# A layout change in a fused attention and MLP kernel: q_p turned by VectorE and DMA from the ninth pair on

## The chip, the cores and the metric

The kernel runs on one core of a Trainium2 chip. The metric is the device time in microseconds of one execution, the median of several runs; smaller is better. Engines: PE is TensorE, PEld its weight loads, DVE is VectorE, ACT is ScalarE, POOL is GpSimd, SP is the engine that issues all DMAs of this kernel.

## What is computed

Attention with positive random features for 8 x 8 (batch, head) slices of 576 tokens and 64 dimensions, and on its output, seen as 4608 tokens of 512 features, an MLP with 2048 hidden units and ELU. q, k, v and omega are fp32, the MLP's weights arrive as fp64.

```
scale = 1 / sqrt(sqrt(D))                       # D = 64, m = 128 features
phi(x): h = x @ omega.T - sum(x*x)/2            # x is q*scale or k*scale
        exp(h - max(h)) / sqrt(m)
q_p, k_p = phi(q * scale), phi(k * scale)       # [576, 128] per head
kv  = k_p.T @ v                                 # [128, 64]
z   = sum over tokens of k_p                    # [128]
num = q_p @ kv
den = q_p @ z + 1e-6
attn = num / den                                # -> x [4608, 512]
out  = elu(x @ w_in) @ w_out                    # [4608, 512] fp32
```

## The kernel before

**Pairs.** The attention is done in 32 pairs of two heads of one batch element, four pairs to a batch element. For pair i, `load_pair` issues the DMAs of k, q and v; `project` (once for k, once for q) makes the nine [128, 128] slices of k_p or q_p, tokens on partitions, in a tile `h` of shape [128, 9, 128]; `kv` makes kv (tile `kvf`) and the sums z; and `finish` does the rest. Of the nine slices of q_p, slices 0, 2, 4, 6 are the first 512 tokens of one head, 1, 3, 5, 7 those of the other, and slice 8 holds the last 64 tokens of both heads, one in each half of the partitions.

**The step that the change touches, `finish` (from L648).** pz (L664) spreads z over the partitions by a matmul. For three groups of slices (four, four, one) VectorE computes the denominators (L685) and reciprocals (L694), and POOL, or sometimes VectorE, multiplies q_p by them (`norm`, L696; the line shown in the profile is that of the helper, L359). Then the normalised q_p has to stand with features on partitions. Before, TensorE transposes each of the nine slices against an identity into PSUM tiles `pt` (L706), and ScalarE (or VectorE) copies each group out into `qh` [128, 2, 576] (L721; shown as L354). At last four matmuls (L733) multiply `kvf` by `qh`, one for each head and each of the token ranges 0..255 and 256..575, into two PSUM tiles `pn`; ScalarE writes the high part `xh` and VectorE the low part `xl` of x, features on partitions, into a ring of two batch elements, for the MLP. `qh` has one buffer, PSUM tiles of tag `pa` three, `h` four, and a tag `raw` (fp64 weights as they arrive, and the tile of the sums z) four.

**The MLP.** x is taken in 12 blocks of 384 tokens. A step of a block takes one of 16 slices of 128 hidden units: `layer1` (L864 to L866: high x high, high x low, low x high, for four feature chunks), ELU on ScalarE and VectorE, a split of the result in g (L882 to L891), and `layer2` (L902 to L904) into three PSUM accumulators. The first three blocks are run in two halves of 8 steps. A step's weights are converted from fp64 once, in the first block, stored to DRAM and loaded again by a DMA of 512 KB for each later step (`weights`, L839), into one of three buffers `w1c`.

**What sets the order.** No engine's order is written by hand. Every piece of work is a task with an engine (or alternatives), an estimated duration, a due time, and the buffers that it reads and writes (`Plan.op`). `Plan.order` runs a simulated clock: whenever an engine is free, it starts, of the tasks whose inputs are ready by that clock and for which buffers are free, the one with the earliest due time. The order so found is then issued, each engine's queue in that order; on the chip every instruction waits for its inputs by semaphores, in its place in the queue. In the plan a task on SP takes 500 ns per DMA, and its data land 1.1 us, plus the bytes at 360 per ns, plus 1.1 us after its start (L118, L244). `pair` (L752) sets the due times: a pair has a due time for its end, and its loads, projections, kv and last steps are due by fixed spans ahead of it. From the ninth pair on (i >= 8) these are the spans `LOAD2, K2, KV2, Q2`. The pairs of batch element b stand spread over the segment of the MLP ahead of the block that first needs them, four to a segment; PE takes MLP tasks and pair tasks in turn, by due time. The ninth to the thirty-second pair are computed while blocks of the MLP run.

Of the kernel before, what the change touches and what calls it, by code (L numbers as in the profile page):

```python
# [9 lines left out]
F32 = mybir.dt.float32  # L10
# [8 lines left out]
P = 128  # L19
B, H, S, D, M = 8, 8, 576, 64, 128  # L20
# [11 lines left out]
NJ = 9  # L32
# [18 lines left out]

PAIR0 = 9.46
DUE_LOAD, DUE_K, DUE_KV, DUE_Q = 27.64, 24.71, 14.12, 18.02
LOAD2, K2, KV2, Q2 = 56.0, 46.17, 30.64, 29.89
TAIL = 11.71
TAIL2 = 4.06

# [10 lines left out]
NHALF = 3  # L68

DUE_Z = 12.0  # L70


NONES = 8
# [27 lines left out]
class Plan:  # L101
# [21 lines left out]
    def op(self, eng, ns, due, fn, reads=(), writes=(), nbytes=0, alt=None, port=False, after=0.0):  # L123
        n = len(self.tasks)
        engs = {eng: (ns, 0.0)}
        for e, *t in alt or ():
            engs[e] = tuple(t)
        f = fn if alt is not None else lambda e: fn()
        deps, bufs = set(), set()
        for k in reads:  # L130
            if k in self.writer:
                deps.add(self.writer[k])
            self.readers.setdefault(k, []).append(n)
        for k in writes:
            if k in self.writer:
                deps.add(self.writer[k])
            deps.update(self.readers.pop(k, ()))
            self.writer[k] = n
        for k in (*reads, *writes):
            b = k[0] if isinstance(k, tuple) else k  # L140
            if isinstance(b, Buf):
                bufs.add(b)
        deps.discard(n)
        for b in bufs:
            b.left += 1
        self.tasks.append((engs, due, f, deps, bufs, nbytes, port, after))
# [135 lines left out]
def mm(n, m=1):  # L282

    return m * (n / 2.23 + 2.5)
# [6 lines left out]
def dve(n, fast=False):  # L291
    return 69 + n / (1.92 if fast else 0.96)
# [7 lines left out]
def performer_elu_kernel(  # L300
# [14 lines left out]
    nc = tc.nc  # L315
# [3 lines left out]
    sb = ctx.enter_context(tc.tile_pool(name="sb", bufs=1))  # L319
# [79 lines left out]
    def bank(i, early, name):  # L399

        tag = early if i < NEARLY else "pa"
        return Buf(ps, [P, 512], F32, tag, name, dict(pa=3, ph=2).get(tag, 1))

    def load_pair(i, due):
        s = st.setdefault(i, {})

        def dma(dst, src, nbytes, *writes):
            nonlocal due
            op("SP", 500, due, lambda: nc.sync.dma_start(dst(), src), (), writes, nbytes)
            due += 0.01  # L410

        for nm, nat, mixed in (("k", k, kx), ("q", q, qx)):
            if native(i, nm):
                t = s["x" + nm] = Buf(sb, [P, 2, S], F32, "ld" if nm == "k" else "t", f"x{nm}_{i}", 3 if nm == "k" else 2)
                dma(lambda t=t: t()[0:D], nat[i], 2 * P * S * 4, (t, 0), (t, 1))
            else:
                t = s["x" + nm] = Buf(sb, [P, 2, S], F32, "ld", f"x{nm}_{i}", 3)
                dma(lambda t=t: t(), mixed[i - NNAT[nm]], P * S * 8, (t, 0), (t, 3))
        t = s["v"] = Buf(sb, [P, NV], F32, "v", f"v_{i}", 2)
        dma(lambda: t(), v[i], P * NV * 4, t)  # L420

    def small(tag, n, name):
        return Buf(sb, [P, n], F32, tag, name, 2)
# [224 lines left out]
    def finish(i, due):  # L648

        s = st[i]  # L650
        h, z = s["hq"], s["z"]
        b, hp = divmod(i, NHP)
        den = small("den", NJ, f"den_{i}")


        pz = bank(i, "ph", f"pz_{i}")

        def spread():
            for a in range(2):
                nc.tensor.transpose(pz()[:, a * P:(a + 1) * P], z()[:, a:a + 1].to_broadcast([P, P]), ident)  # L660

        def sums():
            for e in range(2):
                nc.tensor.matmul(  # L664
                    pz()[:, 0:2 * M], ones, s["zr"]()[:, e * 2 * M:(e + 1) * 2 * M], start=(e == 0), stop=(e == 1)
                )

        if i < NONES:
            op("PE", 220, due - DUE_Z, spread, (z,), (pz,))
        else:  # L670
            op("PE", mm(2 * M, 2), due - DUE_Z, sums, ((s["zr"], "h"), (s["zr"], "l")), (pz,))
        qh = Buf(sb, [P, 2, S], F32, "qh", f"qh_{i}", 1)
        for g in range(3):
            d = due - 9 + g
            js = slice(4 * g, min(4 * g + 4, NJ))
            n = js.stop - js.start
            slots = [(j, j % 2, slice(0, P)) for j in range(4 * g, 4 * g + 4)]
            if g == 2:
                slots = [(8, a, slice(a * D, a * D + D)) for a in range(2)]
            hg = (h, g) if native(i, "q") else (h, min(g, 1))  # L680

            def dens(slots=slots):
                for j, a, r in slots:
                    junk = Buf(sb, [P, M], F32, "junk", f"junk_{i}_{j}_{a}", 2)
                    nc.vector.tensor_tensor_reduce(  # L685
                        out=junk()[r], in0=h()[r, j, :], in1=pz()[r, a * P:(a + 1) * P], scale=1.0, scalar=EPS,
                        op0=ALU.mult, op1=ALU.add, accum_out=den()[r, j:j + 1],
                    )

            def dg(js=js):  # L690
                return den()[:, js]

            op("DVE", len(slots) * 290, d, dens, (hg, pz), ((den, g),))
            op("DVE", 100, d + 0.5, lambda dg=dg: nc.vector.reciprocal(dg(), dg()), ((den, g),), ((den, g),))  # L694
            op(
                "POOL", 145 + 214 * n, d + 1.2,  # L696
                lambda e, js=js, n=n: tt(
                    e, h()[:, js], h()[:, js], den()[:, js].unsqueeze(2).to_broadcast([P, n, M]), ALU.mult
                ),
                (hg, (den, g)), ((h, "n", g),), alt=other("norm", "DVE", dve(n * M)), port=True,  # L700
            )
            p = bank(i, "pa", f"pt_{i}_{g}")

            def turn(g=g, p=p, js=js):
                for e, j in enumerate(range(js.start, js.stop)):
                    nc.tensor.transpose(p()[:, e * P:(e + 1) * P], h()[:, j, :], ident)  # L706

            def src(g=g, p=p):
                if g == 2:
                    return p()[:, 0:P].rearrange("p (a x) -> p a x", a=2)  # L710
                return p().rearrange("p (t a x) -> p a t x", t=2, a=2)

            def dst(x, g=g):
                if g == 2:
                    return x[:, :, 512:S]
                return x[:, :, g * 256:(g + 1) * 256].rearrange("p a (t x) -> p a t x", t=2)

            d = due - 5 + g
            op("PE", 109 * n, d, turn, ((h, "n", g),), (p,))
            op(  # L720
                "ACT", act(n * P, True), d + 0.5, lambda e, src=src, dst=dst: copy(e, dst(qh()), src()), (p,), ((qh, g),),  # L721
                alt=other("turn", "DVE", dve(n * P)),
            )
        kvf = kvs[i % 2]
        halves = [(slice(o, o + n), n, bank(i, "pa", f"pn_{i}_{o}")) for o, n in ((0, 256), (256, S - 256))]

        def mms():
            for qs, n, p in halves:  # L730
                for a in range(2):
                    r = slice(a * D, a * D + D)
                    nc.tensor.matmul(p()[r, 0:n], kvf[:, r], qh()[:, a, qs], start=True, stop=True)  # L733

        d = due - 2
        op("PE", 4 * mm(S) + 200, d, mms, [*((qh, g) for g in range(3)), ("kvf", i % 2)], [p for _, _, p in halves])
        for half, (qs, n, p) in enumerate(halves):
            xs = slice(qs.start + (b % 2) * S, qs.stop + (b % 2) * S)
            key = (b % 2, hp, half)
            op(  # L740
                "ACT", act(n, True), d + 0.8 + half, lambda e, xs=xs, n=n, p=p: copy(e, xh[:, hp, xs], p()[:, 0:n]),
                (p,), (("xh", key),), alt=other("x_hi", "DVE", dve(n)),
            )
            op(
                "DVE", dve(n), d + 1.2 + half,
                lambda xs=xs, n=n, p=p: nc.vector.tensor_tensor(  # L746
                    xl[:, hp, xs], p()[:, 0:n], xh[:, hp, xs].bitcast(F32), ALU.subtract
                ),
                (p, ("xh", key)), (("xl", key),),
            )  # L750

    def pair(i, due):  # L752

        at = (DUE_LOAD, DUE_K, DUE_KV, DUE_Q) if i < 2 * NHP else (LOAD2, K2, KV2, Q2)
        load_pair(i, due - at[0])
        project(i, "k", due - at[1])
        kv(i, due - at[2])
        project(i, "q", due - at[3])
        finish(i, due)


# [292 lines left out]
```

## Time and profile before

| | |
|---|---|
| timed runs | 1067.93, 1071.39, 1075.22 us; median 1071.39 |
| profiled execution, first to last instruction (span) | 1073.6 us |
| mean granted TensorE clock | 0.989 |
| busy: PE, ACT, DVE, POOL | 1046.5, 736.2, 605.4, 430.1 us |
| transposes of q_p (pt), nine a pair | 288 |
| matmul records of the final product (pn), eight a pair | 256 |
| DMA | 176.92 MB, mean 165 GB/s |

No separate device time is given for the profiled execution; its span lies within the range of the timed runs, 2.2 us above their median.

How to read the rows: a group of instructions stands as line, engine, operation, output<-inputs, shapes and count, then busy time in us and mean ns of one, then the engine's idle time ahead of it and what ended it. A matmul of fp32 operands is seen as two records, one of fp32r (the MLP's, the projections') or a transpose as one. Matmuls are pipelined, so the mean duration of one is longer than the step from one to the next; the chain's rows (start, us, what) show the steps. A wait's row tells who waited, for whom, us in total, how often, and the longest. A row of the windows view has the stretch, its length, busy us of each engine, the granted clock, the DMA engines' busy share and GB/s.

### The profile page before, as it was taken

What the parts mean: (1) busy time and instruction counts of PE and PEld (TensorE: products, weight loads), DVE (VectorE), ACT (ScalarE), POOL (GpSimd) and SP (SyncE); (2) the same over time, 40 slices, a digit from 0 to 9 for tenths busy, and PEclk for the clock granted to TensorE, in tenths of its full rate; (3) what the DMA queues carried; (4) which work ended last, traced back from release to release, by engine and by line L of the source; (5) the groups of instructions that cost most, each with busy time, mean ns of one, the idle gap of its engine ahead of it and who ended that gap; (6) DMA issues with size and microseconds to landing.
All of it is one profiled execution on the core that took longest, in us unless ns stands there. A gap on an engine that the chain in (4) does not pass through costs nothing.

```text
span 1073.6 us, 19168 instructions
## 1 busy us (share of the span) xinstructions
PE 1046.5 (97%) x6043; PEld 917.7 (85%) x6043; DVE 605.4 (56%) x2395; ACT 736.2 (69%) x1972; POOL 430.1 (40%) x440
## 2 busy tenths in 40 slices
PE   8989899999999999999999999999999999999998
PEld 7878789778888888998888888899888888899997
DVE  6898987684676764235556666224566665322221
ACT  6888775774878985347889988427889888432222
POOL 2446434234434563223455345323344454322221
PEclk8999899999999999999999999999999999999999
DMA  5666576558553553534544545443545542353431
GB/s 138 200 206 221 190 264 204 200 205 284 174 186 133 195 170 122 168 118 172 181 158 155 170 150 178 148 137 133 184 136 177 156 143 99 99 167 128 156 123 64
DMA packets 53238, 176.92 MB, mean 165 GB/s; under 512 B 6033, under 2 KB 6225, under 8 KB 53137
## 3 DMA queue, kind: packets, MB, share of 16 engines
q1 hardware_dynamic: 53136, 175.69, 49.5%
q8 instruction: 49, 0.80, 0.3%
q14 instruction: 53, 0.43, 0.1%
HBM read 155.48 MB, written 20.19 MB: 164 GB/s over the span
## 4 chain that ended last, share of the span: by engine, by line
PE 78%; ACT 8%; DVE 5%; DMA 3%; issue 2%; POOL 2%; SPq 0%; ACTq 0%; POOLq 0%; DVEq 0%
PE ph L864 11%; PE acc L902 10%; PE ph L866 10%; PE ph L865 10%; PE acc L903 10%; PE acc L904 10%; PE pn L733 3%; PE pt L706 3%; PE ppq L516 2%; ACT p2k L525 2%; DMA xq<-in_qx_dram 2%; PE pkv L608 2%; PE ppk L516 1%; ACT hk L436 1%; PE ppq L466 1%
## 5 line engine op out<-in xcount | busy, mean ns | idle before, releaser
L359 POOL TENSOR_TENSOR g<-e,g 128x384 fp32r<-128x384 f32 x176 | 187.3, 1065 | 430.9 <-DVE g L356 357.7
L864 PE MATMUL ph<-xh,w1c 128*128 128x384 f32 x768 | 266.4, 347 | 3.0 <-DVE e L877 1.6
L866 PE MATMUL ph<-xh,w1c 128*128 128x384 f32 x768 | 259.9, 338 | 0.9 <-DVE w1c L359 0.9
L865 PE MATMUL ph<-xl,w1c 128*128 128x384 f32 x768 | 259.3, 338 | 0.1
L877 DVE SCALAR_TENSOR_TENSOR e<-e,ph 128x384 f32<-128x384 f32 x192 | 106.2, 553 | 229.0 <-ACT e L874 221.6
L902 PE MATMUL acc<-w2h,g 128*128 128x512 f32 x576 | 231.5, 402 | 0.0
L873 ACT ACTIVATE e<-ph 128x384 f32<-128x384 f32 x192 | 94.4, 492 | 199.0 <-PE ph L866 195.4
L903 PE MATMUL acc<-w2l,g 128*128 128x512 f32 x576 | 227.2, 394 | 0.2 <-DVE w2l L359 0.2
L904 PE MATMUL acc<-w2h,g 128*128 128x512 f32 x576 | 225.5, 392 | 0.0
L864 PEld LDWEIGHTS ph<-xh,w1c 128*128 128x128 f32 x768 | 144.9, 189 | 18.3 <-issue 6.2
L865 PEld LDWEIGHTS ph<-xl,w1c 128*128 128x128 f32 x768 | 145.1, 189 | 7.3 <-DVE xl L746 0.4
L866 PEld LDWEIGHTS ph<-xh,w1c 128*128 128x128 f32 x768 | 144.7, 188 | 1.7 <-DVE w1c L359 1.5
L904 PEld LDWEIGHTS acc<-w2h,g 128*128 128x128 f32 x576 | 108.4, 188 | 24.4
L902 PEld LDWEIGHTS acc<-w2h,g 128*128 128x128 f32 x576 | 108.7, 189 | 16.7 <-issue 3.6
L903 PEld LDWEIGHTS acc<-w2l,g 128*128 128x128 f32 x576 | 108.7, 189 | 11.0 <-DVE w2l L359 0.5
L874 ACT ACTIVATE e<-e 128x384 f32<-128x384 f32 x192 | 101.4, 529 | 3.5
L534 DVE CUSTOM_DVE_ANT_0 hq<-ppq,p2q 128x128 f32<-128x128 f32 x216 | 54.6, 287 | 80.6 <-ACT p2q L525 70.3
L359 POOL TENSOR_TENSOR hq<-hq,den 128x512 f32<-128x512 f32 (+1 forms) x95 | 80.8, 866 | 45.8 <-DVE den L694 34.1
L525 ACT ACTIVATE p2q<-ppq,sqq 128x128 f32<-128x128 f32 x216 | 67.9, 373 | 21.3 <-PE ppq L516 20.9
L534 DVE CUSTOM_DVE_ANT_0 hk<-ppk,p2k 128x128 f32<-128x128 f32 x225 | 56.9, 287 | 40.4 <-ACT p2k L525 33.9
L685 DVE CUSTOM_DVE_ANT_0 junk<-hq,pz 128x128 f32<-128x128 f32 (+1 forms) x320 | 73.7, 280 | 8.7 <-PE pz L664 6.4
L812 POOL TENSOR_TENSOR u_w<-u_w,raw_w 128x512 int32<-128x512 int32 x32 | 44.9, 1405 | 81.6 <-DVE u_w L809 31.8
(96 smaller groups left out, 1613.2 us busy)
## 6 DMA issues: line engine op xcount, KB each, us to landing
w1c<-w1s SPq DMA_DIRECT2D x176, 512.0 KB, 3.3
raw_w<-in_w_dram SPq DMA_DIRECT2D x32, 512.0 KB, 4.6
xk<-in_kx_dram SPq DMA_DIRECT2D x25, 576.0 KB, 4.8
xq<-in_qx_dram SPq DMA_DIRECT2D x24, 576.0 KB, 4.2
v<-in_v_dram SPq DMA_DIRECT2D x32, 325.0 KB, 3.8
out_dram<-o SPq DMA_DIRECT2D x36, 256.0 KB, 3.6
w1s<-w1c SPq DMA_DIRECT2D x16, 512.0 KB, 3.0
xq<-in_q_dram SPq DMA_DIRECT2D x8, 288.0 KB, 4.2
```

What stands on the lines that cost most here:

```text
L359: (nc.vector if e == "DVE" else nc.gpsimd).tensor_tensor(*args)
L525: nc.scalar.activation(p2()[:, a], view()[:, a, M:], AF.Identity, bias=sq()[:, j:j + 1], scale=1.0)
L534: nc.vector.tensor_tensor_reduce(out=h()[:, j, :], in0=view()[:, a, 0:M], in1=p2()[:, a, :], scale=1.0, scalar=HIGHEST, op0=ALU.add, op1=A ...
L864: nc.tensor.matmul(ph(), wh, xh[:, c, o:o + TB], start=(c == 0), stop=False)
L865: nc.tensor.matmul(ph(), wh, xl[:, c, o:o + TB], start=False, stop=False)
L866: nc.tensor.matmul(ph(), wl, xh[:, c, o:o + TB], start=False, stop=(c == NC - 1))
L873: op("ACT", act(TB, True), due, lambda: nc.scalar.activation(e(), ph(), AF.Relu, scale=-1.0), (p,), (e,))
L874: op("ACT", act(TB), due + 0.2, lambda: nc.scalar.activation(e(), e(), AF.Exp, scale=-1.0), (e,), (e,))
L877: lambda: nc.vector.scalar_tensor_tensor(e(), e(), -1.0, ph(), ALU.add, ALU.max), (p, e), (e,),
L902: nc.tensor.matmul(a(), g()[:, 0, ts], w2h[:, f], start=(f == f0), stop=False)
L903: nc.tensor.matmul(a(), g()[:, 0, ts], w2l[:, f], start=False, stop=False)
L904: nc.tensor.matmul(a(), g()[:, 1, ts], w2h[:, f], start=False, stop=(f == f1 - 1))
```

## The change

For the pairs i >= 8 (`TURNED`) the nine transposes, their PSUM tiles and the copies are left out. In their place:

- One VectorE instruction transposes every 32 x 32 block of the nine normalised slices within itself, from `h` into a new tile `tb` [128, 1152] (tag `raw`), ordered so that the 288 columns that go to one group of 32 feature partitions are contiguous.
- Sixteen DMAs, from SBUF to SBUF, move blocks of [32 partitions, 288 columns] (36 KB) from token group n of `tb` to feature group m of `qh`. All 16 are issued on SP's queue, as four tasks of four.
- The columns of `qh` are now ordered by token group, slice and token within the group. The final product reads its tokens in runs of 32 through a strided pattern, and takes 256 columns at most: per head two matmuls of 256 columns and one of 64, where there were one of 256 and one of 320.
- The final product waits for the four move tasks in place of the three copies.
- Due times: the loads, both projections, pz, the denominators and the normalising of these pairs are due 7 us earlier (`EARLIER`); kv is due 33.0 in place of 30.64 us ahead of the pair's end. The end itself is due as before.

The first eight pairs and the MLP are not changed.

```diff
-LOAD2, K2, KV2, Q2 = 56.0, 46.17, 30.64, 29.89
+LOAD2, K2, KV2, Q2 = 56.0, 46.17, 33.0, 29.89
...
+TURNED = 8
+EARLIER = 7.0
+QB = 32
+NQB = P // QB
...
+        early = EARLIER if i >= TURNED else 0.0
...
-            op("PE", mm(2 * M, 2), due - DUE_Z, sums, ((s["zr"], "h"), (s["zr"], "l")), (pz,))
+            op("PE", mm(2 * M, 2), due - DUE_Z - early, sums, ((s["zr"], "h"), (s["zr"], "l")), (pz,))
...
-            d = due - 9 + g
+            d = due - 9 + g - early
...
+            if i >= TURNED:
+                continue
             p = bank(i, "pa", f"pt_{i}_{g}")
...
+        if i >= TURNED:
+            tb = Buf(sb, [P, NQB * NJ * QB], F32, "raw", f"tb_{i}", 4)
+
+            def blocks():
+                nc.vector.transpose(
+                    out=tb().rearrange("p (n j c) -> p j n c", n=NQB, j=NJ),
+                    in_=h().rearrange("p j (n c) -> p j n c", c=QB),
+                )
+
+            op("DVE", dve(NJ * M), due - 10, blocks, [(h, "n", g) for g in range(3)], (tb,))
+            for n in range(NQB):
+
+                def move(n=n):
+                    q = qh().rearrange("p a (n x) -> p (a n) x", n=2)
+                    w = NJ * QB
+                    for m in range(NQB):
+                        nc.sync.dma_start(
+                            q[m * QB:(m + 1) * QB, n], tb()[n * QB:(n + 1) * QB, m * w:(m + 1) * w]
+                        )
+
+                op("SP", 500 * NQB, due - 9, move, (tb,), ((qh, n),), QB * P * NJ * 4)
...
-                    nc.tensor.matmul(p()[r, 0:n], kvf[:, r], qh()[:, a, qs], start=True, stop=True)
+                    if i < TURNED:
+                        nc.tensor.matmul(p()[r, 0:n], kvf[:, r], qh()[:, a, qs], start=True, stop=True)
+                        continue
+                    q = qh().rearrange("p a (n j c) -> p (a n) j c", n=2, j=NJ)
+                    t = qs.start // P
+                    x = q[:, :, 2 * t + a:2 * t + a + 3:2, :].rearrange("p n j c -> p j n c")
+                    nc.tensor.matmul(p()[r, 0:2 * P], kvf[:, r], x, start=True, stop=True)
+                for a in range(2):
+                    if i >= TURNED and n > 2 * P:
+                        r = slice(a * D, a * D + D)
+                        nc.tensor.matmul(
+                            p()[r, 2 * P:n], kvf[:, r], q[:, 2 * a:2 * a + 2, 8, :], start=True, stop=True
+                        )
...
-        op("PE", 4 * mm(S) + 200, d, mms, [*((qh, g) for g in range(3)), ("kvf", i % 2)], [p for _, _, p in halves])
+        parts = range(NQB if i >= TURNED else 3)
+        op("PE", 4 * mm(S) + 200, d, mms, [*((qh, g) for g in parts), ("kvf", i % 2)], [p for _, _, p in halves])
...
-        load_pair(i, due - at[0])
-        project(i, "k", due - at[1])
+        load_pair(i, due - at[0] - (EARLIER if i >= TURNED else 0.0))
+        early = EARLIER if i >= TURNED else 0.0
+        project(i, "k", due - at[1] - early)
         kv(i, due - at[2])
-        project(i, "q", due - at[3])
+        project(i, "q", due - at[3] - early)
```

## The prediction

> **What bounds the kernel now.** I read the page first (busy shares and slices), then the windows view over the stages, then the waits, and last the chain and the timeline around single pairs.
>
> ```profile
> span 1073.6 us, 19168 instructions
> PE 1046.5 (97%) x6043; PEld 917.7 (85%) x6043; DVE 605.4 (56%) x2395; ACT 736.2 (69%) x1972; POOL 430.1 (40%) x440
> ```
>
> TensorE is busy for 97% of the span. A share of the whole span does not tell about a stage, so here are the windows that hold the pairs from the ninth on (their work lies between about 260 and 940 us):
>
> ```profile
> core 0: us, PE busy (x) PEld busy (x) DVE busy (x) ACT busy (x) POOL busy (x), PEclk, DMA share, GB/s
> 260.00:440.00 180.00, 179.65 (x1087) 155.52 (x1087) 108.85 (x515) 140.26 (x392) 78.49 (x83) 1.00 0.52 170
> 440.00:600.00 160.00, 158.95 (x928) 140.06 (x928) 81.78 (x371) 117.27 (x331) 63.89 (x68) 1.00 0.47 154
> 600.00:760.00 160.00, 159.13 (x908) 140.55 (x907) 76.81 (x332) 106.67 (x288) 60.72 (x65) 1.00 0.49 159
> 760.00:940.00 180.00, 178.41 (x1085) 154.30 (x1084) 102.39 (x516) 144.90 (x414) 82.94 (x91) 1.00 0.43 139
> ```
>
> The granted clock is 1.00 in all four, and PE's idle time is 0.35, 1.05, 0.87 and 1.59 us: 3.9 us in 680. So in this stage TensorE sets the pace. What is taken from it is gained, and any time it spends waiting is lost for good. VectorE has about half of each window free, and the DMA engines too.
>
> ```profile
> PE pt L706 <- POOL hq L359: 1.7, 6, 0.3
> PE pt L706 <- ACT qh L354: 1.4, 3, 0.5
> PE ppq L516 <- DVE mnq L534: 0.6, 1, 0.6
> PE ph L864 <- DMA w1c<-w1s: 0.5, 1, 0.5
> ```
>
> These are PE's waits from 250 us on: 3.1 of 4.2 us belong to the transposes that the change takes away, and the weight loads almost never make PE wait.
>
> **What is removed.** Nine transposes in each of 24 pairs are 216 instructions. The group's mean duration (first row below) overlaps with its neighbours, so I take the price from the chain, where only the step to the next matmul counts.
>
> ```profile
> L706 PE MATMUL pt<-ident,hq 128*128 128x128 f32 x288 | 50.2, 287 | 6.3 <-POOL hq L359 4.1 <-ACT qh L354 1.4 <-DVE hq L359 0.4
> 513.81 0.44 PE pt L706 x4
> 336.62 0.11 PE pt L706
> 333.58 1.24 PE pkv L608 x20
> 519.29 1.12 PE pn L733 x8
> ```
>
> 0.44 for four and 0.11 for one give 0.11 us each: 216 x 0.11 = **23.8 us**. With them go their two waits, **3.1 us**. ScalarE loses the copies out of PSUM, 24 x (2 x 590 + 276 ns) = 34.9 us, off the bound:
>
> ```profile
> L354 ACT COPY qh<-pt 128x512 f32<-128x512 f32 x64 | 37.7, 590 | 14.3 <-PE pt L706 14.0
> L354 ACT COPY qh<-pt 128x128 f32<-128x128 f32 x32 | 8.8, 276 | 1.9 <-PE pt L706 1.6
> ```
>
> That costs or gains nothing by itself; without that slack it would be worth 1.45 us a pair. The three PSUM banks of a pair that carried the transposes also fall free.
>
> **What is added on TensorE.** The final product had 2 x 256 and 2 x 320 columns per pair, seen as 8 records in 1.12 us. Now it has 4 x 256 and 2 x 64: the same 1152 columns in 12 records. The rows of 128 columns (pkv, 1.24 us for 20, so 0.062 us each) and of pn (1.12 us for 2304 columns in two passes, 0.49 ns a column) have the same price per column, so no fixed price is seen. Below: nothing extra. Above: a record of 64 columns costs as much as one of 128, 0.031 us more for each of four, 0.12 us a pair, 3.0 us in all. I take the middle, **1.5 us**. The moving operand is now read in runs of 32 floats; no row has that, so a full doubling stands among the rivals.
>
> **What is added elsewhere.** VectorE gets one transpose of 1152 columns per pair. The nearest rows:
>
> ```profile
> L356 DVE CAST g<-e 128x384 fp32r<-128x384 f32 x121 | 45.4, 375 | 23.4 <-PE acc L904 20.5
> L488 DVE TENSOR_REDUCE sqk<-xk 128x9 f32<-128x576 f32 x25 | 18.7, 748 | 12.5 <-ACT xk L485 12.4
> ```
>
> 375/384 and 748/576 ns a column make 1.1 to 1.5 us; I take 1.4. 24 of them are 34 us of VectorE, in windows where it is idle for 71 to 83 us each: nothing as busy time, but it counts in the path below. SP gets 16 issues of 36 KB each per pair, 24 x 0.59 = 14.2 MB. Issue, landing and volume now:
>
> ```profile
> 508.62 0.82 SPq L924 DMA_DIRECT2D out_dram<-o  x2
> 5.02 1.10 SPq L371 DMA_DIRECT2D omf<-in_omT_dram  x2
> 24.54 0.47 SPq L409 DMA_DIRECT2D xq<-in_q_dram  x1
> w1s<-w1c SPq DMA_DIRECT2D x16, 512.0 KB, 3.0
> w1c<-w1s SPq DMA_DIRECT2D x176, 512.0 KB, 3.3
> part<-o SPq DMA_DIRECT2D x9, 256.0 KB, 2.8
> SPq L839 <- PE ph L866: 425.1, 120, 9.6
> L864 PE MATMUL ph<-xh,w1c 128*128 128x384 f32 x768 | 266.4, 347 | 3.0 <-DVE e L877 1.6
> q1 hardware_dynamic: 53136, 175.69, 49.5%
> ```
>
> Two whole-tile stores back to back take 0.41 us each, two 64-row loads at the start 0.55, and one 64-row load alone 0.47. The moves have 32 rows, so I take 0.50, bounds 0.41 and 0.55. From issue to landing out of SBUF the trace has 3.0 us for 512 KB and 2.8 for 256. That bounds 36 KB from above at 3.0; half of it, 1.5, is the lower bound, and I take 2.4, a little under the line through both.
>
> The added volume is 8% of the 176 MB that now take half of the DMA engines' time: hidden. The moves wait on SP for the transpose, and behind them stand weight loads, the next loads of q, k, v and the stores. The weights have three buffers: SP spends 425 us waiting until a buffer is free, so a load is issued about two steps before its use, 2 x 1073.6/192 = 11 us (768 matmuls of L864, four a step, are 192 steps), and lands in 3.3. Sixteen issues, 8 us, would use up what is left only if all stood ahead of a load; the plan puts them by due times between loads. Price nothing; without that cover, up to a microsecond or two a pair. The loads, projections, sums and normalising that move 7 us earlier keep their instructions; their three loads per pair pass weight loads on SP, and the four h buffers are held longer. Price nothing, since PE waits for none of them now; in the ninth to twelfth pair, the closest ones, a few us if the buffers run out.
>
> **The step that decides: when the final product can start.** TensorE runs in the order that the plan wrote, so if the data of pn are late by the clock though not by the plan, PE stands, with the MLP matmuls (L864 to L904) queued behind pn.
>
> ```profile
> 559.98 1.40 POOL L359 TENSOR_TENSOR hq<-hq,den 128x512 f32<-128x512 f32 x2
> 563.96 0.27 ACT L354 COPY qh<-pt 128x128 f32<-128x128 f32 x1
> 565.41 1.19 PE L733 MATMUL pn<-qh,kvf 128*64 128x256 f32 x8
> 580.90 2.92 POOL L359 TENSOR_TENSOR hq<-hq,den 128x512 f32<-128x512 f32 x3
> 585.97 1.14 PE L733 MATMUL pn<-qh,kvf 128*64 128x256 f32 x8
> 604.47 1.41 POOL L359 TENSOR_TENSOR hq<-hq,den 128x512 f32<-128x512 f32 x2
> 612.40 1.19 PE L733 MATMUL pn<-qh,kvf 128*64 128x256 f32 x8
> ```
>
> From the end of the normalising to pn a middle pair of a batch has 4.0 us (561.38 to 565.41), the last one 2.1, the first one 6.5. New: transpose 1.4, hand-overs 0.3, fifteen more issues 7.5, landing 2.4: 11.6 us. The plan itself counts 1.3 for the transpose, 0.3 of hand-overs and 8.6 for the moves (four tasks of 2 us, the last ending 2.6 us after its start): 10.2. The chip is thus 1.4 us behind the plan. The chain starts 7 us earlier, so at its old place in PE's order pn would come 13.5 us after the normalising in a first pair, where the data are there; 11.0 in a middle one, where they are 0.6 late; and 9.1 in a last one, where the plan (10.2) must put pn later and the chip's 1.4 count, less the slack that the middle pair shows: its copy ends at 564.23, pn starts 1.18 later, and the plan asks for 0.27, so 0.9. PE stands 0.5 to 0.6 us; I take 0.5 for the 18 pairs that are not first in a batch: **9.0 us**. With the low ends (1.1 + 0.3 + 6.2 + 1.5 = 9.1 us) nothing remains; with the high ends (1.5 + 0.3 + 8.3 + 3.0 = 13.1) it is 2.0 us, 36 us over 18 pairs.
>
> The Trainium skill, in "DMA: Bandwidth & Descriptors" under "Anatomy of one DMA", gives about 2.0 us as fixed cost of a DMA (for the other descriptor path); with it as landing the standing would be 0.1 to 0.2 us a pair and the sum about 6 us better. No row here has so small a transfer out of SBUF.
>
> **The sum.** -23.8 - 3.1 + 1.5 + 9.0 = -16.4 us. The span of the profiled execution is 1073.6, 2.2 above the median of the runs; the sum is taken from the span, 1057.2, and 2.2 lower for a median: **1055**.
>
> **Rivals.**
> 1. No standing at all. The issues cost 0.41 and landings are short. For it: the plan's slack of 0.9 and ScalarE's relief, which brings the chain ahead. Against it: 64-row DMAs cost more than whole tiles. -23.8 - 3.1 + 1.5 = -25.4: 1046.
> 2. The wait takes the place of the transposes and outweighs them. One mechanism, at pn's first matmul: the moves land later than the plan says. It decides from 25.4/24 = 1.06 us per pair on (1.4 if first pairs are spared). For it: PE has no idle time to absorb it, and the high ends give 2.0: 1071.4 - 25.4 + 36 = 1082 on 18 pairs, 1094 if all 24 stand so long. Against it: first pairs have 1.9 us to spare. The Trainium skill speaks for this side, in "VectorE: DVE Perf Modes" under "Rules for kernel authors": a 128x128 transpose belongs on TensorE where PSUM is a possible destination, VectorE's serves within 32x32. The trace's 0.11 us per transpose agrees that TensorE's is cheap; that it is nevertheless on the bound is what speaks against following it.
> 3. The gain is eaten to within 1%: standing of 0.8 to 1.4 us on 18 pairs, 14 to 25 us, so 1060 to 1071; or the strided operand doubles pn, 24 x 1.12 = 27 us, 1073. For it: all bounds between the taken values and the high ends. Against doubling: pn and pkv are priced by columns alone.
> 4. The transposes were hidden anyway, so nothing changes: 1071. Against it: 3.9 us idle in 680.
>
> **How the numbers follow.** About 1% is what a measurement here can tell from no change (runs of before lie 0.7% apart): below 1060.7 is faster, above 1082.1 slower. Forecast 0.36; rival 1 0.22; rival 3 0.20; rival 4 0.04; rival 2 0.18. Faster 0.58, same 0.24, slower 0.18. The range reaches from just under rival 1 to the lower part of rival 2: 1044 to 1080; the forecast's own is 1048 to 1060.
>
> **What would show it.** L706 x72 instead of x288; PE's busy time from the pairs' stage down by some 22 us; pn x352 in place of x256 (64 for the first eight pairs and 24 x 12) with 1.1 to 1.3 us a pair on the chain; a transpose of 1.1 to 1.5 us x24 on VectorE; 384 new DMAs on SP at 0.4 to 0.55 us each; and a new row in PE's waits, pn waiting for a DMA of qh, of about 9 us. If that row has over 25 us, rival 2 is right; if pn's matmuls take twice as long, rival 3; if PE waits for w1c, the weight loads have lost their cover and a step I priced at nothing is wrong.

## The result and the profile after

The changed kernel takes **1130.74 us** (median of 4 runs, 1125.92 to 1139.97) against 1070.34 us before: a ratio of 1.0573, 95% interval 1.0531 to 1.0614. It is slower by 60 us where 15 us faster was forecast.

The page of the changed kernel (busy us, share of the span, instructions), and the windows of the pairs' stage with the columns as before:

```profile
span 1124.1 us, 19491 instructions
PE 1042.2 (93%) x5923; PEld 918.8 (82%) x5923; DVE 641.4 (57%) x2415; ACT 716.9 (64%) x1905; POOL 429.9 (38%) x439
...
260.00:440.00 180.00, 163.00 (x972) 142.72 (x971) 114.64 (x512) 126.90 (x357) 77.26 (x82) 0.97 0.54 179
440.00:600.00 160.00, 150.25 (x845) 133.42 (x844) 81.23 (x340) 104.43 (x283) 57.17 (x61) 0.97 0.49 164
600.00:760.00 160.00, 147.75 (x823) 130.60 (x822) 79.29 (x314) 92.92 (x250) 56.55 (x62) 0.96 0.48 164
760.00:940.00 180.00, 167.02 (x983) 147.40 (x981) 112.14 (x495) 144.06 (x410) 75.54 (x82) 0.96 0.48 158
```

In these 680 us TensorE is now idle for 52 us (before: 3.9), and its granted clock is 0.96 to 0.97 (before: 1.00). The groups of the changed kernel name the place: line 770 is the final product, line 715 the transposes that are left, line 737 the VectorE transpose, line 749 the moves. The figure after the bar and the mean is the idle time just ahead of the group.

```profile
L770 PE MATMUL pn<-qh,kvf 128*64 128x256 f32 x192 | 30.6, 442 | 52.7 <-DMA qh<-tb 36.2 <-ACT e L918 4.3 <-ACT e L919 3.6
L715 PE MATMUL pt<-ident,hq 128*128 128x128 f32 x72 | 12.5, 294 | 3.1 <-ACT hk L442 2.0 <-POOL hq L365 0.6 <-DVE hq L365 0.3
L737 DVE STREAM_TRANSPOSE tb<-hq 128x1152 f32<-128x1152 f32 x24 | 33.0, 1375 | 6.5 <-POOL hq L365 6.3
qh<-tb SPq DMA_DIRECT2D x384, 36.0 KB, 1.9
```

PE stands 52.7 us ahead of the product: 22 of the 24 pairs stand, for 2.4 us on average, and the ninth and tenth do not. Part of it is put down to ScalarE; but the product reads only `qh` and `kvf`, and one pair in the timelines of SP, VectorE and PE (start, us, what) shows what it waits for:

```profile
628.49 1.38 DVE L737 STREAM_TRANSPOSE tb<-hq 128x1152 f32<-128x1152 f32 x1 [1.25 <-POOL hq L365]
```

```profile
629.90 10.63 SPq L749 DMA_DIRECT2D qh<-tb  x16
```

```profile
639.78 0.34 PE L911 MATMUL ph<-xh,w1c 128*128 128x384 f32 x1
642.30 1.08 PE L770 MATMUL pn<-qh,kvf 128*64 128x256 f32 x8 [2.19 <-ACT e L918]
643.19 0.31 PE L774 MATMUL pn<-qh,kvf 128*64 128x64 f32 x4
```

The sixteen issues alone take 10.6 us, and pn starts 12.4 us after the first of them, 1.8 us after the last has ended. The plan expects the data 8.6 us after the first. In all 22 pairs that stand, pn starts 0.1 to 0.6 us after the last of the sixteen moves has landed, also where the wait is put down to another engine. What follows a stand is seen in narrow windows around two others, one of some 3 us and one of 2:

```profile
586.20:589.40 3.20, 0.37 (x4) 0.08 (x4) 0.48 (x5) 1.09 (x4) 1.00 (x1) 0.97 0.22 59
589.40:592.60 3.20, 3.20 (x16) 2.43 (x17) 0.92 (x2) 1.02 (x3) 0.00 (x0) 0.50 0.97 330
592.60:596.00 3.40, 3.40 (x19) 3.06 (x19) 1.71 (x12) 2.72 (x9) 0.02 (x1) 0.99 0.66 240
```

```profile
613.30:615.20 1.90, 0.15 (x3) 0.04 (x2) 0.87 (x5) 1.78 (x7) 0.87 (x1) 1.00 0.25 70
616.50:619.90 3.40, 3.40 (x11) 2.91 (x12) 1.21 (x6) 0.98 (x3) 0.00 (x0) 0.51 0.97 381
620.00:623.00 3.00, 3.00 (x20) 2.83 (x19) 1.65 (x10) 2.37 (x7) 0.00 (x0) 1.00 0.52 178
```

After each, the granted clock is 0.50 for about 3.4 us; in the second case this begins only after the product. Over the span its mean is 0.970, before 0.989.

The balance of the two spans, from rows: transposes -23.8 and their waits -3.1; the product +1.9 (1.20 us a pair on the chain in place of 1.12); standing +52.7; clock 1124.1 x 0.030 - 1073.6 x 0.011 = +21.9. Together +49.6, seen +50.5. The clock's part is an estimate from the two means. By stages, it was halved for 47.8 us between 260 and 940 us, in fourteen stretches of 3.41 us, which costs 24 us and before cost nothing; ahead of 260 us, where the work is still that of the first eight pairs, it cost about 10 us, before about 12.

### The profile page after: what moved, and what is told of

It reads as the page before. It is cut to its first block, busy times and chain, and to the rows that moved or that the text cites. A ratio compares the mean times of both kernels' runs of the same rounds, so it can differ in the third digit from the quotient of the medians.

```text
span 1124.1 us, 19491 instructions
## 1 busy us (share of the span) xinstructions
PE 1042.2 (93%) x5923; PEld 918.8 (82%) x5923; DVE 641.4 (57%) x2415; ACT 716.9 (64%) x1905; POOL 429.9 (38%) x439
## 4 chain that ended last, share of the span: by engine, by line
PE 58%; ACT 12%; SPq 10%; DMA 8%; DVE 7%; issue 5%; POOL 1%; DVEq 0%; ACTq 0%; POOLq 0%
SPq L749 9%; PE acc L947 8%; PE ph L909 8%; PE acc L948 8%; PE acc L949 8%; PE ph L910 8%; PE ph L911 8%; PE pn L770 2%; DMA qh<-tb 2%; ACT hk L442 2%; ACT hq L442 2%; DMA w1c<-w1s 2%; PE ppk L522 2%; ACT p2k L531 1%; PE ppq L472 1%
## 5 line engine op out<-in xcount | busy, mean ns | idle before, releaser
L365 POOL TENSOR_TENSOR g<-e,g 128x384 fp32r<-128x384 f32 x176 | 183.3, 1042 | 457.8 <-DVE g L362 284.8
L948 PE MATMUL acc<-w2l,g 128*128 128x512 f32 x576 | 230.5, 400 | 0.2 <-DVE w2l L365 0.2
L909 PEld LDWEIGHTS ph<-xh,w1c 128*128 128x128 f32 x768 | 147.1, 191 | 15.5 <-DVE e L922 4.0
L911 PEld LDWEIGHTS ph<-xh,w1c 128*128 128x128 f32 x768 | 146.5, 191 | 1.6 <-DVE w1c L365 1.6
L949 PEld LDWEIGHTS acc<-w2h,g 128*128 128x128 f32 x576 | 110.6, 192 | 25.2
L947 PEld LDWEIGHTS acc<-w2h,g 128*128 128x128 f32 x576 | 110.4, 192 | 17.0 <-issue 2.0
L948 PEld LDWEIGHTS acc<-w2l,g 128*128 128x128 f32 x576 | 110.6, 192 | 12.3 <-DVE w2l L365 0.5
L531 ACT ACTIVATE p2k<-ppk,sqk 128x128 f32<-128x128 f32 x225 | 70.0, 364 | 23.8 <-PE ppk L522 22.9
L770 PE MATMUL pn<-qh,kvf 128*64 128x256 f32 x192 | 30.6, 442 | 52.7 <-DMA qh<-tb 36.2
```

Source lines behind the costliest of these rows:

```text
L365: (nc.vector if e == "DVE" else nc.gpsimd).tensor_tensor(*args)
L531: nc.scalar.activation(p2()[:, a], view()[:, a, M:], AF.Identity, bias=sq()[:, j:j + 1], scale=1.0)
L909: nc.tensor.matmul(ph(), wh, xh[:, c, o:o + TB], start=(c == 0), stop=False)
L911: nc.tensor.matmul(ph(), wl, xh[:, c, o:o + TB], start=False, stop=(c == NC - 1))
L947: nc.tensor.matmul(a(), g()[:, 0, ts], w2h[:, f], start=(f == f0), stop=False)
L948: nc.tensor.matmul(a(), g()[:, 0, ts], w2l[:, f], start=False, stop=False)
```

## The experiments

The theory after the result: SP needs at least 0.63 us for each of sixteen moves, the plan reckons 0.50 and an early landing; so the product stands in PE's queue ahead of its data, and the stands bring the clock down. Rivals: the earlier due times do it; the moves hold up SP's queue and with it the weights; VectorE's transpose or the strided operand cost the time; landings, not issues, are long.

**Four moves in place of sixteen.**

```diff
-                    for m in range(NQB):
-                        nc.sync.dma_start(
-                            q[m * QB:(m + 1) * QB, n], tb()[n * QB:(n + 1) * QB, m * w:(m + 1) * w]
-                        )
+                    nc.sync.dma_start(q[:, n], tb()[:, n * w:(n + 1) * w])
```

> The plan, its order and the amount of data are those of the changed kernel, but each group of four moves of 32 rows is one move of 128 rows and 147 KB, so four DMAs a pair in place of sixteen; the exchange of 32-row groups among partitions is left out, so q_p reaches the wrong features. Theory (SP needs 0.63 us for each of sixteen moves, so qh lands about 3 us later than the plan has it, and TensorE stands at pn): the waits at pn go, TensorE's clock stays at 1.00, and the time is 1045 to 1052 us. Rival (the earlier due times, or the strided operand, or the VectorE transpose cost the time): all of these are still there, so 1110 to 1130.

1044.42 us, ratio 0.9738 (0.9683 to 0.9794), span 1041.1, clock 0.998. The four-move kernel's product, its moves, and the one stage that was worst:

```profile
L767 PE MATMUL pn<-qh,kvf 128*64 128x256 f32 x192 | 26.0, 392 | 0.0
```

```profile
519.30 2.43 SPq L748 DMA_DIRECT2D qh<-tb  x4
```

```profile
600.00:760.00 160.00, 159.94 (x914) 142.95 (x913) 87.44 (x361) 104.91 (x280) 63.66 (x67) 1.00 0.52 172
```

This kernel leaves out the exchange of 32-row groups among partitions, so it prices the wait and is no kernel to use. With the same order on every engine but for twelve issues a pair, all of the loss is gone: standing 52.7 us and clock (33.7 against 2.1 us, from the means) are 84 us, the spans differ by 83 (some 8 of them by the clock ahead of 260 us, where the two kernels do the same). VectorE's transpose, the strided operand and the due times are all still there, so none of them is the cause. The strided operand costs nothing that shows: 392 ns mean for 256 columns, 405 before. A 128-row move takes 0.6 us of SP too (2.43 for four), so it is the number of issues that counts: the last move is issued 1.8 us after the first in place of 10.0.

**The due times alone**, with TensorE turning q_p in all pairs.

```diff
-EARLIER = 7.0
+EARLIER = 5.0
+SWAP = 99
-            if i >= TURNED:
+            if i >= SWAP:
                 continue
...
```

> TensorE turns q_p in all 32 pairs as before the change, but the due times are moved as in the change, by 5 us in place of 7, with kv due at 33.0. Theory: the due times do no harm, 1065 to 1080 us. Rival (the earlier due times fill h and the PSUM banks and break the order): 1100 or more, with waits on PE at other lines than pn.

1075.44 us, ratio 1.001 (0.9976 to 1.0043). The due times by themselves do nothing, at 5 us; with 7 the plan finds no order for this variant that fits its buffers. The four-move kernel has the 7 us and loses nothing.

**The plan's price of a move.** One number is changed, in four kernels.

```diff
-                op("SP", 500 * NQB, due - 9, move, (tb,), ((qh, n),), QB * P * NJ * 4)
+                op("SP", 750 * NQB, due - 9, move, (tb,), ((qh, n),), QB * P * NJ * 4)
```

> The changed kernel with the plan reckoning 350 ns a move in place of 500: its last landing comes 1.8 us earlier, the chip's does not. Theory (pn always stands where the plan has its data ready, so each microsecond between the plan's and the chip's landing is lost in each of 24 pairs): 1.8 us more a pair, 43 us, and some for the clock: 1165 to 1190 us. Rival (due times hold pn back, so the plan's reckoning matters little below 500): 1125 to 1140.

> The changed kernel with the plan reckoning 640 ns a move, the measured issue, and its landing as it is. Last landing by the plan 10.3 us, by the chip 11.4. Theory: 1.1 us less the 0.45 us of slack that the changed kernel shows, 0.6 us a pair, 15 us beside the kernel without waits: 1058 to 1072. If the price of an issue alone were the fault, no wait is left: 1045 to 1052.

> The changed kernel with one number of the plan changed: a move is reckoned at 750 ns of SP in place of 500, so that the plan's last landing, 9.0 + 2.6 = 11.6 us after the first issue, is that of the trace (15 x 0.634 + 1.9 = 11.4). Theory (the loss is the gap between the plan's and the chip's landing, not the moves as such): the plan puts other matmuls ahead of pn, the waits fall from 2.3 us a pair to under 0.7, 1050 to 1065 us. Rival (the moves hold up SP's queue and so the weights, whatever the order): 1090 or more, with waits for w1c.

> The changed kernel with the plan reckoning 850 ns a move: its last landing is 12.8 us after the first issue, 1.4 us after the chip's. Theory: no wait at pn is left, 1046 to 1056 us. Rival (SP's queue, taken for 13.6 us a pair by the plan, moves weight loads back): 1058 to 1075, with waits for w1c.

The groups of the product in the kernels with 350, 640, 750 and 850 ns, in this order:

```profile
L770 PE MATMUL pn<-qh,kvf 128*64 128x256 f32 x192 | 42.8, 588 | 93.3 <-DMA qh<-tb 86.1 <-issue 7.2
```

```profile
L770 PE MATMUL pn<-qh,kvf 128*64 128x256 f32 x192 | 26.5, 394 | 20.0 <-DMA qh<-tb 10.7 <-DVE mnk L540 2.7 <-ACT hk L442 2.5
```

```profile
L770 PE MATMUL pn<-qh,kvf 128*64 128x256 f32 x192 | 26.9, 401 | 7.0 <-DMA qh<-tb 3.9 <-DVE mnk L540 1.7 <-ACT p2k L531 0.7
```

```profile
L770 PE MATMUL pn<-qh,kvf 128*64 128x256 f32 x192 | 26.2, 392 | 2.5 <-DMA qh<-tb 1.6 <-ACT tk L360 0.4 <-DVE mnq L540 0.4
```

| reckoned per move | plan's last landing after the first issue | idle ahead of pn | clock, profiled run | median | ratio |
|---|---|---|---|---|---|
| 350 ns | 6.8 us | 93.3 us | 0.941 | 1188.72 | 1.1095 (1.1041 to 1.115) |
| 500 ns (the change) | 8.6 | 52.7 | 0.970 | 1130.74 | 1.0573 (1.0531 to 1.0614) |
| 640 ns | 10.3 | 20.0 | 0.992 | 1067.27 | 0.9967 (0.9938 to 0.9995) |
| 750 ns | 11.6 | 7.0 | 0.992 | 1058.10 | 0.9868 (0.9811 to 0.9925) |
| 850 ns | 12.8 | 2.5 | 0.989 | 1059.58 | 0.9894 (0.9851 to 0.9937) |

The chip does the same work in all five, in another order: the plan moves the product, and other tasks with it, on every engine. So the standing, which is read at the product alone, is the surer column, and a time of the table can hold other effects of the order. From 500 to 350 the plan's landing moves by 1.8 us and the standing by 40.6 us, 1.85 us on average in the 22 pairs that stand in both: every microsecond that the plan is too early is lost in full. The time moves by 58 us, since the clock falls as well. Three expectations held; that for 850 ns did not: 1059.6 in place of at most 1056, with the standing all but gone and next to no wait for weights (0.3 us in the pairs' stage). Its rival gave the time, but by waits for weights that are not there.

**Steps due still earlier.**

```diff
-EARLIER = 7.0
+EARLIER = 10.0
```

> The changed kernel with the early steps of the ninth and later pairs due 10 us ahead in place of 7; the plan still reckons 500 ns for a move. Theory: in first and middle pairs pn then stands 14 us and more behind the normalising in PE's order, past the 13.1 us that the chip needs, so their waits go; last pairs keep up to 1 us. 1045 to 1058 us. Rival (the chip is always behind the plan, however early the chain starts, since the plan starts the chain's end as soon as it can): waits as in the changed kernel, 1110 to 1130.

1122.57 us, ratio 1.0473 (1.0403 to 1.0543), 50.9 us idle ahead of pn: the rival was right. Two rows of this kernel, SP's moves and the product of the same pair as above, the twenty-first:

```profile
622.61 10.49 SPq L749 DMA_DIRECT2D qh<-tb  x16
```

```profile
634.94 1.08 PE L770 MATMUL pn<-qh,kvf 128*64 128x256 f32 x8 [1.09 <-DMA qh<-tb]
```

Again pn starts 12.3 us after the first move. The due time does not hold the product back; the plan puts it where it has the data ready, and starting the chain earlier moves the product along with it.

**Both: 750 ns and 9 us.**

```diff
-EARLIER = 7.0
+EARLIER = 9.0
-                op("SP", 500 * NQB, due - 9, move, (tb,), ((qh, n),), QB * P * NJ * 4)
+                op("SP", 750 * NQB, due - 9, move, (tb,), ((qh, n),), QB * P * NJ * 4)
```

> The changed kernel with the plan reckoning 750 ns a move and the early steps due 9 us ahead in place of 7. Theory: no pair's product waits for its moves, and none comes later than before the change, so the time is that of the four-move kernel without a wait, 1042 to 1052 us, less than the 1058.1 with 7 us. Rival (earlier steps hold h and the weights' buffers longer and cost as much as they save): 1055 to 1065.

1058.53 us, ratio 0.9885 (0.9832 to 0.9939), 5.9 us idle ahead of pn: no better than with 7 us, and the expectation failed. The time is the rival's; its reason, buffers held longer, is not shown by this run.

**The stand filled with work.**

```diff
+NFILL = 10
...
+            for _ in range(NFILL if i >= TURNED else 0):
+                nc.tensor.matmul(halves[0][2]()[:, 0:P], ident, ident, start=True, stop=True)
             for qs, n, p in halves:
```

> The changed kernel with ten matmuls of identity by identity ahead of pn in each of the 24 pairs, written into pn's bank and overwritten there, so that TensorE works for about 2 us of the stand and not for its result. Theory with a clock part (after most stands the granted clock is halved for 3.4 us, worth 10 to 15 us in all): the clock mean goes from 0.97 to 0.98 or more and the time falls by 5 to 15 us against the changed kernel, to 1115 to 1125. Without such a part (the halved stretches cost nothing beside the stand): 1130 to 1140, since the filling runs past the end of some stands.

1112.22 us, ratio 1.0397 (1.0316 to 1.0477), clock 0.994 in the profiled run, 1.00 in all the pairs' windows. The filling is this group:

```profile
L763 PE MATMUL pn<-ident 128*128 128x128 f32 x480 | 57.4, 275 | 0.0
```

Its 57.4 us and the 9.8 us still idle ahead of pn take more of TensorE than the stands did (52.7), and the order is otherwise that of the changed kernel; yet the kernel is 18.5 us faster. So the halved clock is a loss of its own, beside the standing. About 3 us of the difference between the profiled runs lie ahead of 260 us, where the two kernels do the same; what is left, some 15 us, is an estimate of the least that this loss can be, and the halved stretches themselves give 24. The rest, 68 us above the four-move kernel, is mostly the filling and the idle time.

**The queue's time without the lateness.**

```diff
-            for n in range(NQB):
...
+            def move():
...
+                for n in range(NQB):
+                    nc.sync.dma_start(q[:, n], tb()[:, n * w:(n + 1) * w])
+
+            op("SP", 640 * NQB, due - 9, move, (tb,), [(qh, n) for n in range(NQB)], 2 * NQB * QB * P * NJ * 4)
+            for n in range(NQB - 1):
+
+                def idle(n=n):
...
                         nc.sync.dma_start(
-                            q[m * QB:(m + 1) * QB, n], tb()[n * QB:(n + 1) * QB, m * w:(m + 1) * w]
+                            spare[m * QB:(m + 1) * QB, n], tb()[n * QB:(n + 1) * QB, m * w:(m + 1) * w]
                         )
...
-                op("SP", 500 * NQB, due - 9, move, (tb,), ((qh, n),), QB * P * NJ * 4)
+                op("SP", 640 * NQB, due - 9 + 0.1 * (n + 1), idle, (tb,), (("spare", n),), QB * P * NJ * 4)
```

> Four moves of 128 rows fill qh, as in the four-move kernel (the exchange among partitions is left out), and behind them SP issues twelve more moves of 32 rows to DRAM, which nothing waits for. SP is taken as long as in the changed kernel, but the product's data do not come late. Theory (only the lateness of the product's data costs; the queue's time does not): 1042 to 1050 us. Rival (the queue that is taken for 10 us a pair delays weight loads and loads of q and k and explains the 14 us between the four-move kernel and the best plan): 1054 to 1062.

1043.89 us, ratio 0.9738 (0.9685 to 0.9791). The twelve issues to a spare place in DRAM come behind the four moves, so SP spends as many issues as in the changed kernel, and it costs nothing that shows. So the queue's time does not explain why the best plan stays 14 us above the four-move kernel.

**Other ways to send the data.** Every second move on ScalarE's queue:

```diff
+                for eng, issuer in (("SP", nc.sync), ("ACT", nc.scalar)):
...
-                        nc.sync.dma_start(
...
+                        for m in range(eng == "ACT", NQB, 2):
+                            issuer.dma_start(
...
-                op("SP", 500 * NQB, due - 9, move, (tb,), ((qh, n),), QB * P * NJ * 4)
+                    op(eng, 640 * NQB // 2, due - 9, move, (tb,), ((qh, n, eng),), QB * P * NJ * 2)
```

> The changed kernel with every second move issued on ScalarE's queue, the plan reckoning 640 ns a move on each. Theory: two queues issue eight moves in 8 x 0.63 = 5.1 us side by side, so q_p lands about 7 us after the first issue, pn does not wait, but ScalarE loses 5 us a pair to issuing, 121 us in all against the 300 that it has free: 1045 to 1065 us. Rival (the descriptor work is shared by the queues, so the issues slow each other): issues of 1.2 us each, waits at pn as in the changed kernel, 1100 or more.

1094.81 us, ratio 1.0196 (1.0132 to 1.0261); the expectation failed, and so did its rival. ScalarE's and SP's timelines of one pair, and PE's longest wait in this kernel:

```profile
547.55 5.50 ACTq L750 DMA_DIRECT2D qh<-tb  x8
553.09 0.41 ACT L647 CAST zr<-zs 128x256 fp32r<-128x256 f32 x1 [5.41 <-DMA qh<-tb]
```

```profile
547.54 5.17 SPq L750 DMA_DIRECT2D qh<-tb  x8
```

```profile
PE ph L910 <- DVE e L923: 16.1, 8, 3.8
```

The two queues do run side by side at 0.65 and 0.69 us an issue. But ScalarE stands for 5.4 us in one piece while it issues. The waits of TensorE for the MLP's ELU (e), 16.1 us, are 3.2 us in the kernel with 640 ns and one queue; that ScalarE's issuing makes them fits, and is not shown pair by pair. Another 17.8 us of standing are left at the product.

Through DRAM, with one write of 128 rows and four reads of 32 rows:

```diff
+            bd = turned[i % 2]
+            op("SP", 500, due - 9.5, lambda: nc.sync.dma_start(bd, tb()), (tb,), (("bd", i % 2),), P * NQB * NJ * QB * 4)
             for n in range(NQB):
...
-                        nc.sync.dma_start(
...
-                op("SP", 500 * NQB, due - 9, move, (tb,), ((qh, n),), QB * P * NJ * 4)
+                    src = bd.rearrange("(n r) (m x) -> m r n x", n=NQB, m=NQB)
+                    nc.sync.dma_start(q[n * QB:(n + 1) * QB], src[n])
+
+                op("SP", 600, due - 9, move, (("bd", i % 2),), ((qh, n),), QB * P * NJ * 4)
```

> The changed kernel with five DMAs a pair in place of sixteen: one of 128 rows writes tb to DRAM, and four of 32 rows, each with four runs of 1152 bytes a row, read it back as q_p turned. The output is the reference's. On the chip two landings follow each other: 0.6 + 3 for the write, 4 x 0.6 + 2.5 for the reads, 8.5 us in all, about what the plan reckons for it. Theory (the count of issues makes the lateness): waits at pn under 0.5 us a pair, 1043 to 1056 us. Rival (any way through DMA is late by 2 us or more, landings and not issues): 1085 or more.

1074.99 us, ratio 1.0032 (0.9997 to 1.0067): neither. This kernel's DMA rows and its product:

```profile
turned<-tb SPq DMA_DIRECT2D x24, 576.0 KB, 4.7
qh<-turned SPq DMA_DIRECT2D x96, 144.0 KB, 4.1
```

```profile
L770 PE MATMUL pn<-qh,kvf 128*64 128x256 f32 x192 | 27.2, 404 | 19.7 <-DMA qh<-turned 11.1 <-DVE mnk L541 4.1 <-ACT e L919 1.5
```

Two landings of 4.7 and 4.1 us one after the other are longer than the 3 and 2.5 that I had put in, and 19.7 us of standing are left, where under 12 (0.5 us a pair) were expected.

**The best version** that computes what the reference does is the change with 750 ns a move: 1058.10 us, 0.9868 of before. The kernel with 850 ns and that with 750 ns and 9 us lie within 1.5 us of it, too close to tell apart.

## Why the prediction was wrong

What bounds the kernel was right: what was taken from TensorE in the pairs' stage was gained (the four-move kernel, 29 us below its own runs of before, where the terms -23.8 - 3.1 + 1.9 give 25; the scatter of the clock ahead of 260 us, below, is larger than the rest), and what it waited there was lost. Of the terms, the transposes and their waits, the product (+1.5 forecast, +1.9 seen) and VectorE's transpose (1.4 forecast, 1.375 seen) were right, and weight loads never held TensorE. The mechanism of rival 2 is what happened. **The step that failed is the standing ahead of the product: 0.5 us in 18 pairs, 9.0 us, was forecast; 52.7 us, 2.4 us in 22 pairs, is what came, and a lower clock behind it that had no term at all.** It failed in three places.

1. *The issue's price.* I took 0.50 us with 0.55 as the high end; over the 24 pairs it is 0.63 to 0.71 (0.67 in the pair shown), so fifteen of them make 1.9 to 3.1 us more than I had. The lowest of these values stood in the trace of before, in the first loads, which nothing holds up:

```profile
1.36 0.58 SPq L362 DMA_DIRECT2D of<-in_omT_dram  x1
1.99 0.59 SPq L409 DMA_DIRECT2D xq<-in_q_dram  x1
2.62 0.58 SPq L409 DMA_DIRECT2D v<-in_v_dram  x1
3.25 0.47 SPq L409 DMA_DIRECT2D xk<-in_k_dram  x1
```

Their starts are 0.63 us apart. I had read durations, of rows with one or two DMAs; for a series the distance of the starts counts. The landing that I took (2.4) was longer than the 1.9 of the rows after, and gave back 0.5.

2. *First pairs are not spared.* I let due times hold the product at its old place in the order, 11.0 to 13.5 us after the normalising. The kernel with 10 us shows that they do not: pn stands 12.3 us after the first move, at 10 us as at 7. The plan puts it at its own landing, so a pair pays the difference between the plan's landing and the chip's, less the time by which TensorE itself is behind the plan. In the pair shown the plan has the data 8.6 us after the first move; TensorE came to the product at 10.2 (639.78 + 0.34), and pn started at 12.4, after standing 2.2. Of the six first pairs of a batch five stand, for 1.9 to 3.5 us; only the ninth pair does not. The table of prices shows the same from 350 to 850 ns.

3. *The clock was left out.* Its mean fell from 0.989 to 0.970, 22 us between the two spans; the halved stretches of the pairs' stage make 24 us, and the filled kernel shows at least some 15 us of it by itself. With 52.7 us in place of 9.0 the forecast's own sum would have been 1071.4 - 25.4 + 52.7 = 1099; the clock makes up most of the rest to 1130.7. No rival had it, and so even rival 2's 1094 lies far below. The Trainium skill, in "TensorE: Matmul & The Clock Gate" under "Why this matters for your kernels", warns of idle gaps of more than about 3 us between bursts of matmuls; the trace agrees after the stand of 3 us at 586.20 and differs twice: the clock was also halved after the stand of about 2 us at 613.30, and not after one of 3.3 us.

Which stands bring the clock down can be read from the changed kernel's trace. Between 260 and 940 us the halved stretches start at times that differ by whole multiples of 3.413 us (398.09, 589.23 and 616.54 among them), so the span can be cut into stretches on that one grid. Two stands, of 2.1 us (up to 398.10) and of 3.3 us (up to 327.94), in such stretches and the next:

```profile
394.68:398.09 3.41, 1.30 (x7) 0.85 (x6) 1.67 (x10) 2.60 (x9) 0.62 (x1) 1.00 0.31 71
398.09:401.51 3.42, 3.41 (x16) 2.47 (x17) 1.42 (x5) 1.47 (x4) 1.00 (x1) 0.50 0.94 314
```

```profile
323.00:326.41 3.41, 1.65 (x9) 1.14 (x7) 2.28 (x12) 2.77 (x9) 3.33 (x4) 1.00 0.24 63
326.41:329.82 3.41, 1.88 (x16) 1.67 (x17) 0.62 (x3) 1.01 (x3) 2.08 (x3) 1.00 0.75 256
329.82:333.23 3.41, 3.41 (x25) 2.86 (x25) 2.35 (x9) 2.07 (x7) 2.63 (x4) 1.00 0.69 262
```

The shorter stand lies within one stretch, 2.11 us of it, and the next stretch is halved; the longer one is cut into 1.76 and 1.53 us, and none is. In all of the pairs' stage, each of the ten stretches with 1.87 us of idle time or more is followed by a halved one, of five with 1.75 to 1.86 us three are, and below that none, but for one stretch that was itself halved. So what counts here is the idle time within one stretch, a little over half of it, and not the length of the stand.

The 15 us by which the plan with 850 ns, with no standing left, stays above the four-move kernel are 17.8 us between the profiled spans. In the pairs' stage PE's windows show 7.7 us more of idle time (669.9 us busy against 677.6 in 680), 4.9 us of it waits for e, and a clock of 1.00 in both. The rest lies ahead of it, in the first 260 us of the two kernels, 850 ns first:

```profile
0.00:260.00 260.00, 237.83 (x1391) 206.63 (x1392) 204.14 (x600) 190.12 (x481) 113.72 (x104) 0.95 0.63 208
```

```profile
0.00:260.00 260.00, 238.68 (x1439) 206.84 (x1440) 211.56 (x618) 194.43 (x498) 115.40 (x105) 0.99 0.64 214
```

The clock is 0.95 against 0.99, about 10 us. It is not the plan's order: the changed kernel and the filled one have the four-move kernel's order, and the halved stretches there cost them 10 and 7 us, the four-move kernel 2. So some 10 us between two profiled runs can be this scatter. What makes it, and why e comes late in the plan with 850 ns, stay open.

## What to carry to other kernels

Where an order is fixed ahead of time, a wrong price of one step isn't an error of that step's size on its own engine: where the price is too low, the engine that bounds the kernel stands for the difference, each time; a price that was too high (850 ns) cost nothing that shows. So measure a step's price in the series in which it will run (here sixteen issues in a row), and put it into the plan before judging the change: the same change is 5.7% slower with 500 ns in the plan and 1.3% faster with 750. When work is moved off TensorE on to DMAs, count issues and the landings that follow one another ahead of bytes, and add to any stand of TensorE what the clock takes after it.

## What was not expected of the hardware

- An issue of a DMA on SP has much the same price for 36 KB in 32 rows and for 144 KB in 128 rows, 0.63 to 0.71 and 0.61 us from start to start in a series, where a single load of 512 KB (w1c) keeps SP for 0.32 to 0.34 us. ScalarE's queue issues beside it at 0.69 us.
- 36 KB from SBUF to SBUF land 1.9 us after their issue, 144 KB 2.7 us (median, four-move kernel), and a write to DRAM of 576 KB and a read from it of 144 KB 4.7 and 4.1 (the kernel through DRAM).
- A stand of TensorE of 2 to 3 us can be followed by 3.4 us at half its clock, if some 1.8 us of it fall into one stretch of 3.41 us on a grid that is fixed within the run; filling the stand with ten useless matmuls a pair makes the kernel 18.5 us faster.
- A moving operand in runs of 32 floats costs no more than a contiguous one (392 ns for 256 columns in the four-move kernel, 405 before).
